# Hash attention, then a gated feed-forward: the first head prepared in two parts, and a new order for batch 0

## The chip, the cores and the metric

One core of a Trainium2 chip runs the whole program. The core has five engines with queues of their own: PE (TensorE: matrix products into PSUM), DVE (VectorE), ACT (ScalarE: exponential, Gelu, Tanh), POOL (GpSimd) and SP (SyncE, which here only issues DMA). Each engine runs its instructions in the order in which the program wrote them; between engines there are semaphores. The metric is the device time of one execution in microseconds, lower is better.

## The reference

There are four batches of eight heads, 768 tokens and 64 numbers a token. Every query and key gets six hash bits, the signs of its products with `proj`; a query attends only to the keys that have the same six bits.

```python
q_bits = (np.einsum('bhsd,dk->bhsk', q, proj) > 0).astype(np.int64)
k_bits = (np.einsum('bhsd,dk->bhsk', k, proj) > 0).astype(np.int64)
q_bucket = np.sum(q_bits * powers, axis=-1)
k_bucket = np.sum(k_bits * powers, axis=-1)
mask = q_bucket[:, :, :, None] == k_bucket[:, :, None, :]
scores = np.where(mask, scale * np.matmul(q, k.transpose(0, 1, 3, 2)), -1000000000.0)
attn = np.exp(scores - np.max(scores, axis=-1, keepdims=True))
attn = attn / (np.sum(attn, axis=-1, keepdims=True) + 1e-09)
attn_out = np.matmul(attn, v).astype(np.float32)
# x: the heads of a token side by side, 3072 x 512
ffn_out = gelu(x @ w_gate) * (x @ w_val) @ w_out
out = x + ffn_out / (1.0 + np.exp(-(x @ w_res)))
```

## The kernel before

Heads go in pairs: sixteen pairs, four to a batch. A head is 128 partitions by six stripes of 64 numbers (token = partition times six plus stripe). For a pair and a side (q or k) the steps are these. `load` brings the fp32 numbers into a tile `ld`. `tr` turns each 32 x 32 square on DVE (line 240) into a tile `t32`. The hash is a product with `proj` on PE in fp32, of which the trace shows two instructions for each product: `hash_one` does one head alone with a block-diagonal `projs` (line 298), `hash_mm` several pairs jointly (line 251). `bits_one` (lines 304 and 306), or `hash_tok` and `bits` (lines 271 and 287), turn the result back and write plus or minus a half per bit into columns 64 to 69 of a bf16 tile `nat`, beside the 64 numbers that `cast` (lines 206 to 210) put there and a constant column. PE then transposes `nat` stripe by stripe into PSUM (`turn_pe`, line 351), and `turned` copies that into `aug` (lines 358 and 360), where tokens lie along the free dimension. So a score of equal bits comes out higher than any other by a large margin, and the exponential needs no mask.

`scores(p, c)` makes one score tile of 128 x 1024 for pair p, chunk c (line 479), and ACT takes its exponential (line 490). A pair has nine chunks. Two score tiles fit in PSUM (`sc_ps`), so a score waits until the exponential two before it is done. `values` multiplies a chunk by v (line 452), and `finish` divides by the sums on DVE (lines 403 and 404) and writes `x_tok`, which is turned into `x_sb` by DMA or, for the last two pairs of batch 0, by PE (`x_turn`, line 436). Two accumulators `av_ps` exist for `hash_one`, `values` and some turns.

The feed-forward part of a batch is `gate_val` (twelve steps m of 2.6 us; two products on PE at line 503, Gelu at line 520, their product `hh` on DVE at line 523) and `project` (lines 535 and 551), which is spread over the next batch's scores.

Batch 0's attention has no earlier work to lie beside. Its order is written out by hand in the string `ORDER`: every word is a job, issued in that order on whichever engines it uses. `s7` is the score of chunk 7 counted over the batch (nine to a pair), `v7` its values, `tr31` the DVE transpose of pair 3's k, `h12` the third piece of the joint hash 1 (pairs 2 and 3), `tk1` its tokens, `bt`, `tp`, `td`, `cs` the bits, PE turn, copy and cast of a pair and side, `ld` and `lv` loads, `va` and `vs` the preparation of v on POOL, `fin31` a `finish`, `w0` to `w11` the slices of the four weight matrices (issued on POOL), `xt` an `x_turn`, `g0` and `g1` the first part of `gate_val`'s first step. `BESIDE` lists what follows each of the twelve steps m of batch 0's `gate_val`; `tu` there is a turn by DMA. Batches 1 to 3 are placed by a loop with fixed slots; with `FROM = 1` it makes the hash of half the pairs of the following batch on POOL and DVE, for b of 1 and more.

Ahead of `ORDER`, the program loads head 0 of q and k (lines 128 and 131; `projn` goes on ACT's queue between them), head 1, and then `FIRST_LOADS`, all on SP. It sets constants, runs filler products on PE (`fill`, line 174), transposes and hashes head 0 of q, then of k, and turns each (lines 564 to 586). The first score needs stripes 0 to 3 of q and stripes 0 and 1 of k; the second needs the rest of q and stripes 0 to 2 of k.

Of the kernel before, what the change touches and what calls it, by code (L numbers as in the profile page):

```python
# [9 lines left out]
FP32 = mybir.dt.float32  # L10
# [14 lines left out]
td200 v13 fin10 bt31 s17 ld51 va4 v14 s18 tr50 tp201 w0 w1 w2 bt30 td201 s19 v15 vs2 s20 tp211 cs41  # L25
td211 s21 v16 v17 cs40 s22 tr61 v18 v19 tr40 w3 s23 va3 tp310 td310 tr60 s24 v20 tp300 td300 ld70
s25 vs3 v21 tp301 td301 s26 vs4 fin11 s27 v22 v23 fin20 tr41 s28 v24 v25 s29 tp311 td311 s30 v26
# [3 lines left out]
BESIDE = [  # L31
    "h23 tk2 bt41",
    "tu41 cs61 bt40",
    "bt50",
    "tu40 cs60 ld71 tr71",
    "tr70",
    "tu50 bt51 w8 w9",
    "",
    "w10",
    "h30 h31 h32 h33 tu51 cs71 tk3 bt60 bt61 tu60 tu61",  # L40
    "pr40 rp40 bt71 tu71",
    "bt70",
    "w11 cs70 tu70",
]

@with_exitstack
def kernel(
# [44 lines left out]
    va_pool = ctx.enter_context(tc.tile_pool(name="va", bufs=4))  # L92
    e_pool = ctx.enter_context(tc.tile_pool(name="e", bufs=4))
    sm_pool = ctx.enter_context(tc.tile_pool(name="sm", bufs=2))
    sc_ps = ctx.enter_context(tc.tile_pool(name="sc_ps", bufs=2, space=PSUM))
    av_ps = ctx.enter_context(tc.tile_pool(name="av_ps", bufs=2, space=PSUM))
    mm_ps = ctx.enter_context(tc.tile_pool(name="mm_ps", bufs=1, space=PSUM))
# [27 lines left out]
        eng.dma_start(raw[p, side][:, hi * T:(hi + 1) * T].rearrange("p t d -> p (t d)"),  # L125
                      (q, k)[side][b, 2 * hp + hi].rearrange("(p t) d -> p (t d)", t=T))
# [4 lines left out]
    load_head(0, 1, 0, nc.sync)  # L131
    load_head(0, 0, 1, nc.sync)
    load_head(0, 1, 1, nc.sync)
    for what in FIRST_LOADS:
# [20 lines left out]
    def blank(i, eng):  # L155
        nat.append(const.tile([P, HT, P], BF16, name=f"nat{i}"))
        eng.memset(nat[i][:, :, D:P], 0.0)
        eng.memset(nat[i][:, :, D + NBITS:KA], 1.0 if i % 2 == 0 else -NBITS / 4.0)

    for i in range(NN):  # L160
        blank(i, nc.vector)

    def spread(dst, engs):
        for a, eng in enumerate(engs):
# [32 lines left out]
    def nat_of(x):  # L197
        return nat[(2 * x[0] + x[1]) % NN]

    def cast(p, side, eng, h0=0, h1=2):  # L200
# [8 lines left out]
        else:  # L209
            eng.tensor_copy(dst, raw[x][:, sl])  # L210

    t32, hsum, htok = {}, {}, {}
    free_banks, held_banks = ["r", "f"], {}

# [21 lines left out]
    def tr(p, side, h0=0, h1=2):  # L236
        if (p, side) not in t32:
# [2 lines left out]
        nc.vector.transpose(t32[p, side][:, sl].rearrange("p c h n -> p (c h n)"),  # L240
                            raw[p, side][:, sl].rearrange("p c d -> p (c d)"))

    def hash_mm(jobs, dhs=(0, 1), hs_=(0, 1)):
        if jobs[0] not in hsum:
            hsum[jobs[0]] = mm_ps.tile([P, HT, 32], FP32, tag=take(jobs[0]), name="hs")
        hs = hsum[jobs[0]]
        for hh in hs_:
            sl = slice(hh * T, hh * T + T)
            for dh in dhs:
                for j, x in enumerate(jobs):  # L250
                    nc.tensor.matmul(hs[32 * j:32 * j + 32, sl], projw[:, dh, :],  # L251
                                     t32[x][:, sl, dh, :], start=(dh == 0), stop=(dh == 1),
                                     tile_position=(0, 32 * j))
# [11 lines left out]
    def hash_tok(jobs, psum=False):  # L265
        n = 32 * len(jobs)
        if psum:
            ht = mm_ps.tile([P, HT, 32], FP32, tag=take(("ht", ht_of(jobs))), name="htp")
        else:
            ht = sm_pool.tile([P, HT + 3, 32], FP32, tag="ht", name="ht")  # L270
# [31 lines left out]
    def bits_one(p, side, hi):  # L302
        hs = hsum.pop((p, side, hi))
        nc.vector.transpose(hs[:, 1].rearrange("p c n -> p (c n)"),
                            hs[:, 0].rearrange("p c n -> p (c n)"))
        nc.vector.tensor_scalar(nat_of((p, side))[:, hi * T:hi * T + T, D:D + NBITS],
                                hs[:, 1, :, 0:NBITS], 0.0, 0.5, op0=ALU.is_gt, op1=ALU.subtract)
        acc_done(("hs", p, side, hi))

# [44 lines left out]
    def turned(p, side, hi, eng, t0=0, t1=T):  # L354
        dst = aug[p, side][0:KA, hi * T + t0:hi * T + t1, :]
        pt = pts[p, side, hi][0:KA, t0:t1]
        if eng is nc.scalar:
            nc.scalar.activation(dst, pt, AF.Copy)
        else:
            eng.tensor_copy(dst, pt)  # L360
        if t1 == T:
            give((p, side, hi))
            if ("pt", p, side, hi) in accs:
                acc_done(("pt", p, side, hi))

    def vals_a(p):
        vs = rawv[p]
# [161 lines left out]
    def project(b):  # L529
        hh = hidden[b]  # L530
        for t in range(T):
# [30 lines left out]


    fill(7)
    fill(1, 256)
    spread(lambda a: projs[32 * a:32 * a + 32, :, 32 * a:32 * a + NBITS],
           (nc.gpsimd, nc.scalar, nc.scalar, nc.gpsimd))
    for side in range(2):
        tr(0, side, 0, 1)
        hash_one(0, side, 0, av_ps, "av")  # L570
    cast(0, 0, nc.scalar, 0, 1)
    cast(0, 1, nc.gpsimd, 0, 1)
    bits_one(0, 0, 0)
    turn_pe(0, 0, 0)
    fill(2, 256)
    bits_one(0, 1, 0)
    turned(0, 0, 0, nc.scalar, 0, 4)
    turn_pe(0, 1, 0)
    turned(0, 1, 0, nc.vector, 0, 2)
    for side in range(2):  # L580
        cast(0, side, nc.gpsimd, 1, 2)
    cast(1, 0, nc.gpsimd)
# [61 lines left out]
    def job(name, fn):  # L644
        first[name] = fn
# [13 lines left out]
    job("tdk", lambda: turned(0, 1, 0, nc.vector, 2, T))  # L659
    job("tdq", lambda: turned(0, 0, 0, nc.vector, 4, T))  # L660
# [39 lines left out]
    FROM = 1  # L700
    PROD = (0, 0, 0, 0, 0, 1, 2, 2, 6, 7, 8, 8, 10, 10, 10, 12, 13, 13, 13, 19, 19, 20, 22, 27)
    SUMS = (1, 2, 2, 4, 5, 6, 7, 8, 9, 10, 10, 11, 12, 12, 13, 17, 19, 21, 21, 23, 23, 29, 30, 31)
    CASTS = (2, 5, 10, 11)
    VALS = (9, 6)
    LAYS = (0, 0, 3, 5)
# [4 lines left out]
    for b in range(B - 1):  # L710
        s0, p0 = b * NSLOT, (b + 1) * HP
        xs = [(p0 + i, side) for i in range(2) for side in range(2)]
        ys = [(p0 + 2 + i, side) for i in range(2) for side in range(2)]
        if b > 0:
            for j, (x, y) in enumerate(zip(xs, ys)):
                at(s0 + 24 + 2 * j, lambda x=x: tr(*x))
                at(s0 + 25 + 2 * j, lambda x=x: cast(*x, nc.gpsimd))
                loads(s0 + 2 + 4 * j, (x[0], "qk"[x[1]]))
                loads(s0 + 18 + 3 * j, (y[0], "qk"[y[1]]))
            gv(b, 0, lambda p0=p0: tokens((p0, p0 + 1), True))  # L720
            for m, x in zip(LAYS, xs):
                lay(b, m, x)
            for m, y in zip(CASTS, ys):
                gv(b, m, lambda y=y: cast(*y, nc.gpsimd))
        else:
            for m, names in enumerate(BESIDE):
                for name in names.split():
                    gv(b, m, first.pop(name))
        if b >= FROM:
            s1 = s0 + NSLOT  # L730

            def put(n, piece):
                if n < KF:
                    gv(b, n, piece)
                else:
                    at(s1 + n - KF, piece)

            plan = []
            for i, (y, j) in enumerate((y, j) for y in ys for j in range(NBITS)):
                plan.append((PROD[i] + .3, lambda y=y, j=j: part(y, j)))  # L740
                plan.append((SUMS[i] + .2, lambda y=y, j=j: part_sum(y, j)))
                if j == NBITS - 1:
                    plan.append((SUMS[i] + .2, lambda y=y: (bits_sum(y), turn(*y))))
            for n, piece in sorted(plan, key=lambda e: e[0]):
                put(int(n), piece)
    for p in range(HP, NPAIR):
        if p >= HP + 1:
            at(9 * p - VALS[0], lambda p=p: vals_s(p))
# [82 lines left out]
```

## Time and profile before

| | before |
|---|---|
| median of 3 runs | 342.24 us (340.98 to 342.32) |
| profiled execution | 342.38 us, span 340.7 us |
| PE busy | 331.5 us, 97% of the span |
| DVE, ACT, POOL busy | 217.6, 206.3, 170.1 us |
| first score on PE, first exponential on ACT | 8.77 us, 9.41 us |
| DMA, mean of the span | 126 GB/s |

Times in the views are microseconds from the start of the span. In rows of the view in order of time the columns are: start, duration, engine, line, operation, output and inputs with their shapes, number of instructions, and in brackets the idle time before them and what ended it. SPq and POOLq are queues that issue DMA. In rows of groups: busy time, mean ns of one, idle time before. In rows of waits: total, times, longest.

### The profile page before, as it was taken

The numbers are of one execution on the slowest core, as the hardware profiler recorded it, in microseconds if no ns is written. First come the engines' busy times: TensorE is split into PE (matmuls) and PEld (weight loads), VectorE is DVE, ScalarE is ACT, GpSimd is POOL, SyncE is SP. The second block draws the span as 40 slices with busy tenths as digits, with TensorE's granted clock in tenths as the row PEclk, the third lists the DMA queues.
The fourth block names the chain that finished last, engine by engine and source line by source line (L and its number), as shares of the span: only waits on it lengthen the run. The fifth ranks groups of instructions, "written<-read, shape, count | busy, mean of one in ns | idle before, by whom it ended". The sixth has DMA issues, their size and how long they took to land.

```text
span 340.7 us, 7546 instructions
## 1 busy us (share of the span) xinstructions
PE 331.5 (97%) x3012; PEld 204.2 (60%) x3060; DVE 217.6 (64%) x420; ACT 206.3 (61%) x232; POOL 170.1 (50%) x211
## 2 busy tenths in 40 slices
PE   8999999999999999999999999999999999999995
PEld 5677765555666665555666665556566665665444
DVE  5988737656343847788897675887897444333343
ACT  3689972225999972324999982223999994322220
POOL 4687940320566205998999803998998000000000
PEclk9999999999999999999999999999999999999999
DMA  7949999989786743550487932552251430000012
GB/s 239 378 104 262 171 229 163 179 137 189 178 189 186 228 102 76 101 95 2 94 204 235 258 104 85 94 93 45 48 134 48 100 56 33 31 0 2 31 63 93
DMA packets 71459, 43.09 MB, mean 126 GB/s; under 512 B 49536, under 2 KB 68480, under 8 KB 71424
## 3 DMA queue, kind: packets, MB, share of 16 engines
q1 hardware_dynamic: 65008, 37.37, 43.4%
q0 software_dynamic: 6336, 5.24, 10.5%
q8 instruction: 24, 0.39, 0.5%
q14 instruction: 11, 0.09, 0.1%
q10 hardware_dynamic: 80, 0.00, 0.0%
HBM read 29.56 MB, written 6.29 MB: 105 GB/s over the span
## 4 chain that ended last, share of the span: by engine, by line
PE 87%; ACT 4%; DVE 3%; DMA 2%; issue 2%; SPq 1%; POOL 0%; DVEq 0%
PE sp L503 32%; PE fps L551 17%; PE sp L479 17%; PE av L452 9%; PE rps L535 6%; ACT hh L490 3%; PE hs L251 2%; DVE hh L523 1%; DMA ld<-in_q_dram 1%; DMA ld<-in_k_dram 1%; PE pt L351 1%; DVE nat L287 1%; SPq L125 0%; ACT gt L520 0%; PE hs L298 0%
## 5 line engine op out<-in xcount | busy, mean ns | idle before, releaser
L490 ACT ACTIVATE e<-sp 128x1024 bf16<-128x1024 f32 x108 | 109.1, 1028 | 8.0 <-PE sp L479 2.8
L324 POOL TENSOR_TENSOR pd<-ld,prow 128x768 f32<-128x768 f32 x48 | 86.2, 1815 | 38.5 <-PE hs L251 34.4
L520 ACT ACTIVATE gt<-sp 128x768 bf16<-128x768 f32 x48 | 38.9, 811 | 90.4 <-PE sp L503 90.4
L479 PE MATMUL sp<-aug,aug 71*128 71x256 bf16 (+1 forms) x384 | 85.6, 325 | 0.8 <-DVE aug L360 0.4
L551 PE MATMUL fps<-wo,hh 128*128 128x512 bf16 (+2 forms) x288 | 74.5, 361 | 1.2
L503 PE MATMUL sp<-x_sb,wv 128*128 128x256 bf16 (+1 forms) x375 | 70.4, 324 | 1.3 <-DVE hh L523 0.8
L503 PE MATMUL sp<-x_sb,wg 128*128 128x512 bf16 (+1 forms) x375 | 70.5, 325 | 0.6
L523 DVE TENSOR_TENSOR hh<-gt,sp 128x768 bf16<-128x768 bf16 x48 | 45.8, 953 | 38.6 <-PE sp L503 34.3
L452 PEld LDWEIGHTS <-e 128*128 128x128 bf16 x864 | 40.2, 97 | 25.1
L503 PEld LDWEIGHTS <-wv 128*128 128x128 bf16 x384 | 37.5, 98 | 26.1 <-issue 1.4
L503 PEld LDWEIGHTS <-wg 128*128 128x128 bf16 x384 | 36.9, 98 | 25.7 <-issue 1.7
L328 DVE TENSOR_REDUCE hsum<-pd 128x12 f32<-128x768 f32 x48 | 44.4, 943 | 0.5
L452 PE MATMUL av<-va,e 128*128 128x65 bf16 x864 | 43.4, 193 | 0.1
L551 PEld LDWEIGHTS <-hh 128*128 128x128 bf16 x312 | 28.1, 97 | 21.8
L490 ACT ACTIVATE hh<-sp 128x1024 bf16<-128x1024 f32 x36 | 34.4, 1025 | 4.1 <-PE sp L479 3.9
L479 PEld LDWEIGHTS <-aug 71*128 71x128 bf16 x384 | 29.2, 97 | 11.6 <-issue 2.0
L554 DVE SCALAR_TENSOR_TENSOR fps<-th,fps 128x512 f32<-128x512 f32 (+2 forms) x26 | 16.9, 650 | 28.1 <-PE fps L551 26.7
L431 DVE COPY av<-av 128x390 f32<-128x390 f32 x24 | 13.7, 571 | 20.4 <-PE av L427 20.4
L535 PE MATMUL rps<-wr,x_sb 128*128 128x512 bf16 x90 | 25.9, 378 | 0.3
L210 POOL CAST nat<-ld 128x768 bf16<-128x768 f32 (+1 forms) x17 | 13.4, 788 | 24.2 <-DMA aug<-nat 23.8
L539 ACT ACTIVATE th<-rps 128x512 f32<-128x512 f32 x24 | 14.3, 594 | 18.5 <-PE rps L535 18.5
L240 DVE STREAM_TRANSPOSE t<-ld 128x768 f32<-128x768 f32 (+1 forms) x26 | 22.8, 895 | 1.6 <-DMA ld<-in_k_dram 1.4
(68 smaller groups left out, 260.1 us busy)
## 6 DMA issues: line engine op xcount, KB each, us to landing
ldv<-in_v_dram SPq DMA_DIRECT2D x16, 384.0 KB, 5.1
out_dram<-o SPq DMA_DIRECT2D x23, 256.0 KB, 2.1
ld<-in_q_dram SPq DMA_DIRECT2D x15, 384.0 KB, 4.9
ld<-in_k_dram SPq DMA_DIRECT2D x15, 384.0 KB, 5.3
wg<-in_moe_w_gate_dram POOLq DMA_DIRECT2D x4, 384.0 KB, 7.8
wv<-in_moe_w_val_dram POOLq DMA_DIRECT2D x4, 384.0 KB, 7.8
wo<-in_moe_w_out_dram POOLq DMA_DIRECT2D x3, 512.0 KB, 9.2
wr<-in_moe_w_res_dram POOLq DMA_DIRECT2D x1, 512.0 KB, 7.5
```

The source lines that it names most:

```text
L240: nc.vector.transpose(t32[p, side][:, sl].rearrange("p c h n -> p (c h n)"), raw[p, side][:, sl].rearrange("p c d -> p (c d)"))
L324: nc.gpsimd.tensor_mul(pd, raw[x], prow[:, j].unsqueeze(1).to_broadcast([P, HT, D]))
L328: nc.vector.tensor_reduce(stripes(hsum6)[:, :, :, j], hparts.pop((x, j)).rearrange("p (a c) d -> p a c d", a=3), axis=mybir.AxisListType.X ...
L452: nc.tensor.matmul(av[p, hi][:, qt, :], e[:, off:off + P], va[:, hi, jt, 0:D + 1], start=first, stop=(p >= HP and jt == T - 1), skip_group ...
L479: nc.tensor.matmul(sp[:, off:off + nq * P], ks[0:KA, hi * T + jt, :], qs[0:KA, hi * T + qt0:hi * T + qt0 + nq, :], start=True, stop=True)
L490: nc.scalar.activation(e, sp, AF.Exp, scale=float(ALPHA))
L503: nc.tensor.matmul(sp[:, c0:c1], w[:, kk, bass.ts(m, P)], xs[:, kk, c0:c1], start=(kk == 0), stop=(kk == KM - 1))
L520: nc.scalar.activation(gt, sp[:, 0:S], AF.Gelu)
L523: nc.vector.tensor_mul(hidden[b][:, m, :], gt, ps[1][:, 0:S])
L535: nc.tensor.matmul(rps, x_sb[b][:, kk, t, :], wr[:, kk, :], start=(kk == 0), stop=(kk == KM - 1))
L551: nc.tensor.matmul(fps[:, cs], hh[:, m, bass.ts(t, P)], wo[:, m, cs], start=(m == 0), stop=(m == KF - 1))
L554: nc.vector.scalar_tensor_tensor(fps[:, cs], th[:, cs], 1.0, fps[:, cs], op0=ALU.add, op1=ALU.mult)
```

## The change

- Head 0's loads are four instead of two: part A is stripes 0 to 3 of q and 0 to 1 of k, part B stripes 4 to 5 of q and 2 to 5 of k. Both parts are six stripes, so each fills one `t32` and one `hash_one`. Part A's loads go out first, then `projn`, then part B's.
- Parts are cast into a new tile `lead` instead of `nat`; both are transposed and hashed back to back, then A's bits, A's turn (in two banks), B's casts, A's copy of q on ACT, B's bits, A's copy of k on DVE. Part B's turn is the new job `tpB` in `ORDER`, its copies are `tdk` and `tdq`.
- Of the fillers, the eighth (half length) and the two between the turns go.
- Two of the four `nat` tiles are set on POOL instead of DVE, and `lead` is set on POOL.
- The hash token tile `ht` has one buffer instead of two.
- `FIRST_LOADS` puts v of pair 1 last; `ORDER` and `BESIDE` are new lists of the same jobs (with `tpB` added).
- New tables `PROD0`, `SUMS0` and `CASTS0` for b = 0 in the placing loop.

```diff
-FIRST_LOADS = [(1, "q"), (0, "v"), (1, "k"), (2, "q"), (2, "k"), (1, "v"), (2, "v"), (3, "k"), (3, "q")]
+FIRST_LOADS = [(1, "q"), (0, "v"), (1, "k"), (2, "q"), (2, "k"), (2, "v"), (3, "k"), (3, "q"), (1, "v")]
...
-trq trk s0 tdq tdk hoq bo0 ho bo1 s1 tr10 s2 tr11 tp011 td011a td011b tp001 v0 td001 v1 s3 h00 h01
-s4 cs21 h02 h03 s5 tr20 ld41 ld40 s6 v2 v3 v4 tr21 s7 tk0 bt10 bt11 tp100 tp110 td100 td110 cs20 s8
-ld50 tp111 s9 tr30 tr31 tp101 td101 fin00 s10 lv3 v5 v6 v7 v8 fin01 s11 va1 vs1 lv4 va2 s12 ld60 h10
-h11 h12 h13 ld61 td111 s13 cs31 v9 s14 v10 v11 v12 s15 cs30 tk1 bt20 bt21 tp210 s16 td210 tp200
...
-fin21 lv6 s31 lv5 cs50 v27 s32 cs51 v28 v29 s33 xt2 v30 tr51 s34 w4 w5 w6 v31 fin30 s35 gelu v32 v33
-v34 g0 v35 fin31 g1 xt3 h20 h21 h22 w7 op40
+trq tpB trk tdq s0 tdk hoq bo0 s1 tr10 ld50 ho bo1 tp001 td001 s2 tp011 td011a tr11 s3 td011b v0 v1
+cs21 tr20 s4 h00 h01 h02 h03 w0 s5 v2 v3 s6 v4 s7 tk0 bt10 bt11 tp100 tp110 td100 td110 ld40 tr31 s8
+tp111 td111 cs31 tr30 tr21 ld61 s9 tp101 td101 s10 cs20 v5 v6 v7 v8 ld41 s11 s12 h10 h11 w1 s13
+fin00 h12 h13 va2 lv3 s14 fin01 ld51 s15 va1 v9 v10 v11 tk1 bt20 bt21 bt31 s16 tp200 td200 cs30 vs1
...
+s32 v28 v29 v30 s33 xt2 s34 v31 fin30 op40 tr41 s35 gelu v32 v33 v34 g0 cs40 tr51 v35 fin31 g1 xt3
+h20 h21 cs50 w4 w5 w6 h22 tr60
...
-    "h23 tk2 bt41",
-    "tu41 cs61 bt40",
-    "bt50",
-    "tu40 cs60 ld71 tr71",
-    "tr70",
...
+    "vs4 h23 tk2 bt41 cs51",
+    "ld71 bt50",
+    "w7 tu41 cs61",
+    "tu50 bt40 tu40 cs60",
+    "w8 w9 tr71",
...
-    load_head(0, 0, 0, nc.sync)
+    PARTS = (((0, 0, 4), (1, 0, 2)), ((0, 4, T), (1, 2, T)))
...
+    def tr_part(i, side):
+        if (0, i) not in t32:
+            t32[0, i] = t32_pool.tile([P, HT, 2, 32], FP32, tag="t32", name="t32")
+        d0, d1, t0, t1 = part_of(i, side)
+        nc.vector.transpose(t32[0, i][:, d0:d1].rearrange("p c h n -> p (c h n)"),
+                            raw[0, side][:, t0:t1].rearrange("p c d -> p (c d)"))
...
+    def turn_part(i, sides, av=False):
+        what = ("part", i, sides)
+        if av:
+            acc(what)
+            pt = av_ps.tile([P, T, P], BF16, tag="av", name="pt")
+        else:
+            pt = mm_ps.tile([P, T, P], BF16, tag=take(what), name="pt")
...
     fill(7)
-    fill(1, 256)
     spread(lambda a: projs[32 * a:32 * a + 32, :, 32 * a:32 * a + NBITS],
            (nc.gpsimd, nc.scalar, nc.scalar, nc.gpsimd))
+    for i in range(2):
+        for side in range(2):
+            tr_part(i, side)
+        hash_one(0, i, 0, av_ps, "av")
+    cast_part(0, 0, nc.scalar)
+    cast_part(0, 1, nc.gpsimd)
     for side in range(2):
-        tr(0, side, 0, 1)
-        hash_one(0, side, 0, av_ps, "av")
-    cast(0, 0, nc.scalar, 0, 1)
-    cast(0, 1, nc.gpsimd, 0, 1)
+        aug[0, side] = aug_pool.tile([P, HT, P], BF16, tag=f"aug{side}", name=f"aug{side}")
     bits_one(0, 0, 0)
-    turn_pe(0, 0, 0)
-    fill(2, 256)
+    turn_part(0, (0,))
+    turn_part(0, (1,))
+    cast_part(1, 0, nc.gpsimd)
+    cast_part(1, 1, nc.gpsimd)
+    turned_part(0, 0, nc.scalar)
     bits_one(0, 1, 0)
-    turned(0, 0, 0, nc.scalar, 0, 4)
-    turn_pe(0, 1, 0)
-    turned(0, 1, 0, nc.vector, 0, 2)
+    turned_part(0, 1, nc.vector)
...
+    PROD0 = (0, 1, 2, 3, 4, 5, 6, 7, 8, 9, 10, 11, 12, 14, 16, 17, 19, 20, 22, 24, 25, 27, 28, 30)
...
-            plan = []
+            plan, prod, sums = [], PROD if b else PROD0, SUMS if b else SUMS0
```

More of the change, by code (lines that the diff above doesn't have):

```diff
@@ L126, in load_head, with load_part @@
                       (q, k)[side][b, 2 * hp + hi].rearrange("(p t) d -> p (t d)", t=T))
-    load_head(0, 0, 0, nc.sync)
+    PARTS = (((0, 0, 4), (1, 0, 2)), ((0, 4, T), (1, 2, T)))
+    def load_part(side, t0, t1):
+        if (0, side) not in raw:
+            raw[0, side] = ld_pool.tile([P, HT, D], FP32, tag=f"ld{side}", name=f"ld{side}")
+        nc.sync.dma_start(raw[0, side][:, t0:t1], (q, k)[side][0, 0].rearrange("(p t) d -> p t d", t=T)[:, t0:t1])
+    for part in PARTS[0]:
+        load_part(*part)
     projn = const.tile([32, 2, NBITS], FP32, name="projn")
     nc.scalar.dma_start(projn, proj.rearrange("(h r) n -> r h n", r=32))
-    load_head(0, 1, 0, nc.sync)
+    for part in PARTS[1]:
+        load_part(*part)
     load_head(0, 0, 1, nc.sync)
@@ L364, in turned, with turned_part @@
                 acc_done(("pt", p, side, hi))
+    part_left, part_pt = {}, {}
+    def turn_part(i, sides, av=False):
[3 more added lines that the diff above has]
+            pt = av_ps.tile([P, T, P], BF16, tag="av", name="pt")
+        else:
+            pt = mm_ps.tile([P, T, P], BF16, tag=take(what), name="pt")
+        part_left[what] = len(sides)
+        for side in sides:
+            d0, d1, _, _ = part_of(i, side)
+            for t in range(d0, d1):
+                nc.tensor.transpose(pt[0:KA, t, :], lead[:, i, t, 0:KA], ident)
+            part_pt[i, side] = (pt, what)
+    def turned_part(i, side, eng):
+        d0, d1, t0, t1 = part_of(i, side)
+        pt, what = part_pt[i, side]
+        dst, src = aug[0, side][0:KA, t0:t1, :], pt[0:KA, d0:d1]
+        if eng is nc.scalar:
+            nc.scalar.activation(dst, src, AF.Copy)
+        else:
+            eng.tensor_copy(dst, src)
+        part_left[what] -= 1
+        if part_left[what] == 0:
+            give(what)
+            if what in accs:
+                acc_done(what)
     def vals_a(p):
@@ L702 @@
     SUMS = (1, 2, 2, 4, 5, 6, 7, 8, 9, 10, 10, 11, 12, 12, 13, 17, 19, 21, 21, 23, 23, 29, 30, 31)
+    PROD0 = (0, 1, 2, 3, 4, 5, 6, 7, 8, 9, 10, 11, 12, 14, 16, 17, 19, 20, 22, 24, 25, 27, 28, 30)
+    SUMS0 = (1, 2, 3, 4, 5, 6, 7, 8, 9, 10, 11, 12, 14, 16, 18, 19, 21, 22, 24, 26, 27, 29, 30, 32)
+    CASTS0 = (3, 5, 8, 10)
     CASTS = (2, 5, 10, 11)
```

59 lines of the change are left out of this document (40 added, 19 removed).

## The prediction

> **What bounds the kernel now.** I read the page first (busy shares, the 40 slices), then the waits of PE, then the start in order of time, then the groups of the first batch, and last the stage between 56 and 66 us.
>
> ```profile
> PE 331.5 (97%) x3012; PEld 204.2 (60%) x3060; DVE 217.6 (64%) x420; ACT 206.3 (61%) x232; POOL 170.1 (50%) x211
> ...
> PE   8999999999999999999999999999999999999995
> ```
> ```profile
> PE sp L503 <- DVE hh L523: 0.8, 3, 0.4
> PE sp L479 <- DVE aug L360: 0.4, 1, 0.4
> PE sp L479 <- ACT hh L490: 0.3, 2, 0.2
> ```
>
> TensorE (PE) is full in every slice but the first and the last, and in the whole span it waits for others for under 2 us (us in total, times, longest; the fill's wait for its zeros is left out). So the time is: when dense PE work begins, plus the PE work, plus its few waits. The change leaves the PE work alone but for three fillers, and it touches only what lies before 82 us. It can win by an earlier start and by fewer waits, and lose by new waits. Here is the start:
>
> ```profile
> 0.81 0.39 SPq L125 DMA_DIRECT2D ld<-in_q_dram  x1
> ...
> 1.06 3.38 PE L174 MATMUL wps<-warm 128*128 128x512 bf16 x8 [1.06 <-POOL warm L138]
> 1.10 0.38 DVE L157 MEMSET nat<- 128x384 uint32 x1
> ...
> 1.26 0.41 SPq L125 DMA_DIRECT2D ld<-in_k_dram  x1
> ...
> 1.72 0.42 SPq L125 DMA_DIRECT2D ld<-in_q_dram  x1
> ...
> 2.19 0.43 SPq L125 DMA_DIRECT2D ld<-in_k_dram  x1
> ...
> 3.31 0.44 POOL L168 COPY projs<-projn 32x12 f32<-32x12 f32 x2 [1.45 <-DMA projn<-in_proj_dram]
> ...
> 3.46 1.04 DVE L240 STREAM_TRANSPOSE t<-ld 128x384 f32<-128x384 f32 x2
> ...
> 4.24 2.84 PE L298 MATMUL hs<-t,projs 128*128 128x192 f32 x8
> ...
> 5.84 0.40 DVE L304 STREAM_TRANSPOSE hs<-hs 128x192 f32<-128x192 f32 x1 [1.34 <-PE hs L298]
> ...
> 6.27 0.20 DVE L306 TENSOR_SCALAR nat<-hs 128x36 bf16<-128x36 f32 x1
> ...
> 6.87 0.55 PE L351 MATMUL pt<-ident,nat 128*71 128x128 bf16 x6
> ...
> 7.46 0.59 ACT L358 ACTIVATE aug<-pt 71x512 bf16<-71x512 bf16 x1 [3.13 <-PE pt L351]
> ...
> 7.89 0.50 PE L351 MATMUL pt<-ident,nat 128*71 128x128 bf16 x6 [0.25 <-POOL nat L208]
> ...
> 8.43 0.29 DVE L360 COPY aug<-pt 71x256 bf16<-71x256 bf16 x1 [0.68 <-PE pt L351]
> 8.64 1.02 DVE L240 STREAM_TRANSPOSE t<-ld 128x384 f32<-128x384 f32 x2
> ...
> 8.77 0.60 PE L479 MATMUL sp<-aug,aug 71*128 71x512 bf16 x2 [0.38 <-DVE aug L360]
> ...
> 9.35 1.54 PE L298 MATMUL hs<-t,projs 128*128 128x192 f32 x8
> ...
> 9.59 0.57 DVE L360 COPY aug<-pt 71x256 bf16<-71x256 bf16 x2
> ...
> 10.72 1.03 PE L479 MATMUL sp<-aug,aug 71*128 71x256 bf16 x6
> ...
> 15.47 1.04 PE L479 MATMUL sp<-aug,aug 71*128 71x512 bf16 x5
> ```
> ```profile
> DMA to landing us min/median/max: 2.5/2.6/2.6
> ...
> DMA to landing us min/median/max: 3.6/3.6/3.7
> ```
>
> The two landing lines are the loads of line 125, the first two issues (head 0) and the next two (head 1). The chain to the first score is load, transpose, hash of q, hash of k, k's bits, PE transpose, copy, score at 8.77. PE runs at half rate at first: eight hash passes take 2.63 us up to 6.87 (0.33 each), and the same eight 1.37 us from 9.35 (0.17 each).
>
> **The start, part by part.** Fillers: seven and a half in 3.18 us up to 4.24 is 0.42 each; without the half filler PE is free at 4.03. Loads: part A (4 stripes of q, 2 of k) goes out first; from 0.81 and 1.26 with the first two issues' 2.5 to 2.6 it lands by 3.4 and, being a third of k, between 3.4 and 3.8; I take 3.5. Transposes: 1.04 us for 12 stripes is 0.087 a stripe; A's six take 0.55, so hash A starts at 4.15 (before: 4.24).
>
> Part B is issued at 1.72 and 2.19. With 2.5 it lands at 4.7; with the 3.7 of the third and fourth issue of now, at 5.9. I take 4.7, because A and B together are the bytes that the first two issues bring now; both ends stay in the range. Then B's transposes (0.55) end at 5.25, ahead of hash A's end at 5.47 (4 x 0.33), and hold nothing. Hash B: 5.47 to 6.79. A's bits are ready earlier: DVE reads a hash 1.60 after its start (4.24 to 5.84) and needs 0.63, so 6.38. PE turns A at 6.79; ACT's copy of q (0.59) ends near 7.9. B's bits: 5.47 + 1.60 + 0.63 = 7.70; k's copy follows on DVE (0.29): 7.99. The turn of B now stands ahead of the first score on PE, at 7.81 for 0.34: first score at 8.15. That is **0.62 earlier** (ends: 0.9 with A at 3.3 and PE warm sooner, nothing with B at 5.9, where hash B starts near 6.4).
>
> But k's second part is queued on DVE behind the two transposes of head 1 (1.02) and q's second part (0.25, then 0.40): the second score can't start before 9.8, and PE has only one hash (0.65) for the 1.2 us between: a new wait of 0.55. The turn of k's head 1 waits for its bits (DVE: 0.60 after 9.75, a 0.97 transpose, 0.60: 11.95) for another 0.3. Adding PE's pieces from 9.8 up to the sixth score (three scores 0.43, hash 0.65, two turns 0.34, two value groups 0.24, the list's first joint hash 1.5) gives 15.3 against the 15.47 above: **0.17 of the 0.62 is left**.
>
> Costed at nothing: the memsets moved to POOL (two of 0.38 and six small ones) lie in POOL's 1.45 us wait for proj; without that cover the hash would move by the rest. Two more issues on SP (0.43 each) put every later load back by at most 0.9. POOL's casts of B have from its landing until 7.7, when its bits are ready; the single buffer for hash tokens is free some 7 us before the second use; the new tables PROD0, SUMS0 and CASTS0 apply to batch 0 only, which the planning loop (FROM = 1) skips.
>
> **The rest of batch 0.** From the groups and the chain:
>
> ```profile
> L490 ACT ACTIVATE hh<-sp 128x1024 bf16<-128x1024 f32 x21 | 19.8, 1027 | 0.1
> ```
> ```profile
> 22.70 1.44 PE hs L251 x32
> ...
> 27.35 0.34 PE pt L351 x6
> ...
> 28.11 0.44 PE sp L479 x3
> 28.54 0.24 PE av L452 x8
> ```
> ```profile
> L240 DVE STREAM_TRANSPOSE t<-ld 128x768 f32<-128x768 f32 x12 | 11.2, 958 | 0.1
> L360 DVE COPY aug<-pt 71x768 bf16<-71x768 bf16 x13 | 6.9, 543 | 2.2 <-PE pt L351 2.2
> ```
>
> From 27.6 to 46.3 ScalarE's exponentials follow each other without a hole, 0.92 apart (a score needs the exponential two before it), and PE fills the gaps with turns, values and hashes. I walked both lists slot by slot with these pieces against that pace (between two scores the turns, values and hashes that the list names; a score not before the exponential two before it is done). From the tenth score on that gives 1.5 us of PE waits for the old list and 1.4 for the new one, in other slots. Two new DVE queues come in. Behind the eighth score DVE has four copies (0.54) and three transposes (0.93) before the second joint hash: ready 0.3 after PE asks, of which the next waits give back 0.1: +0.2. At the end, tr41 and tr51 (0.97 each) now stand between the last two `finish` steps: the last one would end near 47.8, and PE reaches the turn that needs it between 47.45 and 47.8: +0.2 (0 to 0.4). Sum for the rest: -0.1 + 0.2 + 0.2 = +0.3, which eats the 0.17 and 0.1 more.
>
> **The feed-forward stage of batch 0.**
>
> ```profile
> 57.46 0.90 SPq L107 DMA_DIRECT2D ld<-in_k_dram  x1
> ...
> 61.68 0.98 DVE L240 STREAM_TRANSPOSE t<-ld 128x768 f32<-128x768 f32 x1 [1.40 <-DMA ld<-in_k_dram]
> 62.58 0.92 DVE L523 TENSOR_TENSOR hh<-gt,sp 128x768 bf16<-128x768 bf16 x1
> ...
> 63.55 1.46 PE L503 MATMUL sp<-x_sb,wv 128*128 128x512 bf16 x8 [0.43 <-DVE hh L523]
> 63.55 1.07 PEld L503 LDWEIGHTS <-wv 128*128 128x128 bf16 x7 [0.60 <-issue]
> ```
>
> Now the load of pair 7's k waits on SP behind a DMA transpose, its DVE transpose waits for it, the product `hh` behind that comes late, and PE stands. The new list loads it after m = 1 and transposes after m = 4, three groups of 2.6 us apart: the wait goes. PE is idle for 0.43 by its row, and its weight loads stand for 0.60, which counts the restart too: **-0.6**. What is late next: nothing, since no m carries more DVE work beside `hh` (0.95) than 1.5 us except m = 8, whose three hash pieces of DVE (2.4) lie beside a 1.4 us hash run on PE as now. The weight slices are issued earlier or, w4 to w6, a few us later than now, some 15 us before their use.
>
> **Sum.** -0.62 + 0.45 + 0.3 - 0.6 = -0.5 us. The profiled execution took 342.38 (span 340.7 and 1.7 around it), 0.14 over the median 342.24. 342.24 - 0.5 = 341.7; I round down to **341.6**, as the end's 0.2 may be nothing. The runs shown spread over 1.34 us, and eight hash passes at half rate cost 1.26 more than at full rate (2.63 - 1.37), so the spread may be the moment at which PE speeds up.
>
> **A rule against the change.** The Trainium skill, "TensorE: Matmul & The Clock Gate", Part 1, says that the array runs at half clock until a free-running window of about 3.4 us has been busy. The rows agree: half rate through the first hash, full after it. By that rule a hole in PE's work between 4 and 7 us could put full rate off by a whole window, and the sum would be +0.4 instead of -0.5, as the first rival prices it.
>
> **Rivals.** (1) Slower: part B lands at 5.9. Hash B starts near 6.4, A's bits wait behind B's transposes on DVE, PE has a hole of 0.9 just before it speeds up. If it speeds up on time the first score comes at 8.6: 342.1. If the hole delays it to about 10.4, hash, turns, first score and next hash (0.34 + 0.34 + 0.43 + 0.65, near 1.8 us at full rate) take twice as long, less the 0.55 wait that this swallows, and part of the later waits: +0.9 on top, 342.6 to 343.3. For it: the third and fourth issues took 3.6 to 3.7. Against: their bytes came behind 384 KB, B's come behind 192. It decides from a landing after 5.0.
> (2) Faster: the two DVE queues of the early list don't bind (copies finish sooner, head 1 transposes overlap) and the start's 0.62 is kept, the waits of the list fall by 0.8, and the 0.6 falls too: -2.0, 340.2. For it: PE never lacks work, only order. Against: DVE's row at 8.64 shows the same two transposes holding the second score now.
> (3) No gain: the list is paced by ACT from slot 13 on, the start's gain is lost whole, and another late transpose takes the place of the one at 61.68: 342.2 to 342.5. For it: 19.8 us of ACT with 0.1 idle. Against: three groups' distance for the load.
> (4) Slower by the third pair's loads: w0 is issued in the fifth slot instead of the nineteenth and runs beside the first loads. k3 and q3 must be there when DVE comes to them near 19.1 and 20.6; each us later delays the second joint hash by as much. Two us late: 343.8.
>
> **Chances.** Forecast (341.1 to 342.1) 0.44, rival 1 0.19, rival 2 0.18, rival 3 0.10, rival 4 and other new waits of its kind 0.09. The range 340.4 to 343.4 leaves out half of rival 2 and the far ends of 1 and 4. About 0.5% (1.7 us) is what a measurement of this kernel tells from no change: below 340.5 most of rival 2, 0.15; above 343.9 the far ends, 0.17 with what I have overlooked in so long a list; between, 0.68.
>
> **What would show it.** In the profile after: hash A near 4.15 and eight passes without a hole; first score near 8.15, second near 9.8 with an idle PE before it; the joint hash of pairs 2 and 3 waiting for DVE's transpose; the x_tok turn near 48 waiting for `finish`; no PE wait near 63. Wrong would be: a hole between the hashes, full rate only after 10 us, PE waits of over 0.5 us in the list, or unchanged waits for `hh`.

## The result, and the profile after

The changed kernel takes 345.12 us (median, 344.71 to 347.22) against 342.07 us for the kernel before in the same job: ratio 1.0103, interval 1.0074 to 1.0131. It is 3 us slower, where 0.5 us faster was forecast, and lies above the range. The profiled execution took 344.71 us, 2.33 more than that of before, with a span of 343.0 (before 340.7). The times below are from these two profiles where nothing else is said.

| us from the start of the span | before | after | difference |
|---|---|---|---|
| first score on PE | 8.77 | 7.69 | -1.08 |
| first exponential | 9.41 | 8.32 | -1.09 |
| ninth exponential | 19.01 | 18.58 | -0.43 |
| last exponential of batch 0 | 45.46 | 44.93 | -0.53 |
| first Gelu | 50.40 | 49.88 | -0.52 |
| seventh Gelu | 66.34 | 65.24 | -1.10 |
| tenth Gelu | 75.69 | 74.62 | -1.07 |
| twelfth Gelu | 80.92 | 81.82 | +0.90 |
| first exponential of batch 1 | 83.04 | 83.95 | +0.91 |
| twelfth exponential of batch 1 | 95.39 | 97.36 | +1.97 |
| span | 340.7 | 343.0 | +2.3 |

At 75 us the changed kernel is a full microsecond ahead. Two places turn that round: 2.0 us between the tenth and the twelfth Gelu, and 1.1 us in batch 1's first scores. The last 0.3 us arise at the very end, behind the last products, and stay unexplained.

The page of after, busy times and the slices of PE:

```profile
PE 332.9 (97%) x3057; PEld 203.0 (59%) x3057; DVE 216.9 (63%) x418; ACT 206.4 (60%) x232; POOL 172.1 (50%) x221
...
PE   7999999997999999999999999999999999999995
```

The busy times are those of before within 2 us; the first slice has gone from eight to seven, and the tenth (77 to 86 us) has lost its nine. PE's waits of after (us in total, times, longest):

```profile
PE sp L572 <- DVE hh L592: 2.2, 3, 1.8
...
PE av L496 <- POOL vsum L450: 0.9, 1, 0.9
PE pt L390 <- POOL nat L325: 0.5, 1, 0.5
PE pt L418 <- DVE lead L345: 0.5, 1, 0.5
PE hs L336 <- DVE t L278: 0.4, 1, 0.4
```

The first two rows are the two places. First the start, in order of time:

```profile
1.81 0.73 POOL L167 MEMSET nat<- 128x768 bf16 x1
...
3.22 0.64 DVE L278 STREAM_TRANSPOSE t<-ld 128x256 f32<-128x256 f32 x2 [1.00 <-DMA ld<-in_q_dram]
...
3.63 0.43 POOL L189 COPY projs<-projn 32x12 f32<-32x12 f32 x2
...
4.12 0.85 PEld L336 LDWEIGHTS hs<-t,projs 128*128 128x128 f32 x4 [0.79 <-POOL projs L189]
4.12 1.14 PE L336 MATMUL hs<-t,projs 128*128 128x192 f32 x4
...
5.13 0.45 DVE L278 STREAM_TRANSPOSE t<-ld 128x256 f32<-128x256 f32 x1 [0.57 <-DMA ld<-in_k_dram]
...
5.63 0.92 PE L336 MATMUL hs<-t,projs 128*128 128x192 f32 x4 [0.36 <-DVE t L278]
...
7.36 0.50 PE L418 MATMUL pt<-ident,lead 128*71 128x128 bf16 x6 [0.48 <-DVE lead L345]
...
7.69 0.60 PE L548 MATMUL sp<-aug,aug 71*128 71x512 bf16 x2
...
8.78 0.60 PE L548 MATMUL sp<-aug,aug 71*128 71x256 bf16 x3
```

Hash A starts at 4.12 (forecast 4.15), released by POOL's copy of `projs`, which ends at 4.06; part A has been transposed since 3.86. Part B's k lands at 5.10, so hash B waits 0.36 us. The trace's record of the granted clock (the share of full speed that PE is given) begins with full rate, at 4.61; in before it begins at 6.97. The products agree: the four passes of hash A take 1.14 us, those of hash B 0.92. So the first score comes 0.46 us before the forecast. Of this start's 1.09 us, 0.66 is given back by the ninth exponential, in a place that the prediction didn't name:

```profile
15.50 0.96 POOL L214 DMA_DIRECT2D wg<-in_moe_w_gate_dram  x1
...
16.54 0.99 POOL L325 TENSOR_SCALAR nat<-ht 32x72 bf16<-32x72 f32 x2
...
17.58 0.53 PE L390 MATMUL pt<-ident,nat 128*71 128x128 bf16 x6 [0.51 <-POOL nat L325]
```

The weight load `w0`, now in the fifth slot, costs POOL 0.96 us to issue; POOL's half of the next bits stands behind it, and PE's turn behind those.

Now the place at 77 us, in order of time:

```profile
66.05 21.73 SPq L378 DMA_TRANSPOSE aug<-nat  x4
...
74.62 0.81 ACT L589 ACTIVATE gt<-sp 128x768 bf16<-128x768 f32 x1 [3.33 <-PE sp L572]
...
77.00 0.98 DVE L325 TENSOR_SCALAR nat<-htp 32x72 bf16<-32x72 f32 x4 [2.18 <-DMA aug<-nat]
77.09 0.82 POOL L231 CAST nat<-ld 128x768 bf16<-128x768 f32 x1 [10.26 <-issue]
...
77.86 1.48 POOL L214 DMA_DIRECT2D wo<-in_moe_w_out_dram  x2
78.02 0.95 DVE L592 TENSOR_TENSOR hh<-gt,sp 128x768 bf16<-128x768 bf16 x1
...
79.03 1.46 PE L572 MATMUL sp<-x_sb,wv 128*128 128x512 bf16 x8 [1.84 <-DVE hh L592]
```

DVE stands for 2.18 us at `bt71`, which writes bits into a `nat` tile. The new list has `bt71` after step 8; in the old one it stood after step 9, and DVE came to it at 78.51:

```profile
78.51 0.98 DVE L287 TENSOR_SCALAR nat<-htp 32x72 bf16<-32x72 f32 x4
```

There are four `nat` tiles, and this one is still being read by `tu51`, the DMA transpose of pair 5's k. It was issued at 66.05 and landed 10.9 us later, at 76.98. Behind `bt71` on DVE is the product `hh`, which has its Gelu since 75.43, and behind `hh` is PE. The landing of `tu51`, first in after, then in before (there it was issued at 67.1):

```profile
DMA to landing us min/median/max: 10.9/10.9/10.9
```
```profile
DMA to landing us min/median/max: 7.6/7.6/7.6
```

In before it landed at 74.7, almost four microseconds before DVE came to `bt71`. It lands later now because two weight slices go out with it, as the second experiment shows. POOL's rows of after, then of before:

```profile
64.49 0.83 POOL L229 TENSOR_SCALAR nat<-ld 128x768 bf16<-128x768 f32 x1 [5.60 <-DMA aug<-nat]
65.28 0.81 POOL L214 DMA_DIRECT2D wr<-in_moe_w_res_dram  x1
66.08 0.75 POOL L214 DMA_DIRECT2D wo<-in_moe_w_out_dram  x1
```
```profile
60.55 0.81 POOL L193 DMA_DIRECT2D wr<-in_moe_w_res_dram  x1
61.35 1.50 POOL L193 DMA_DIRECT2D wo<-in_moe_w_out_dram  x2
74.91 0.82 POOL L210 CAST nat<-ld 128x768 bf16<-128x768 f32 x1 [12.06 <-DMA aug<-nat]
```

`w8` and `w9` stand in the list a step earlier than before, and are issued 4.7 us later: on POOL they queue behind `cs60`, which waits until `tu40` has read its tile. `w10` (the first of the two at 77.86) comes some 16 us later than before, where it was the second of the two at 61.35: it now queues behind `cs71`, which waits for `tu51` (10.26 us idle; 12.06 in before, with only `w11` behind it).

The second place, batch 1's first scores:

```profile
87.83 0.58 SPq L355 DMA_DIRECT2D pn<-in_proj_dram  x1
...
91.85 0.87 POOL L359 COPY prow<-pn 128x384 f32<-128x384 f32 x1 [11.64 <-DMA pn<-in_proj_dram]
92.70 0.99 POOL L446 TENSOR_TENSOR v<-ldv 128x384 f32<-128x384 f32 x1
...
94.69 0.11 POOL L450 MEMSET vsum<- 128x2 bf16 x1
...
94.85 0.19 PE L496 MATMUL av<-vsum,eps_sb 128*128 128x65 bf16 x1 [0.91 <-POOL vsum L450]
```

The rows of `proj` (`pn`) go out on SP behind the turns; SP issues them at 87.83 (before: 84.0). POOL comes to their copy `prow` 11.64 us before they land, and everything behind it on POOL waits with it, among it the sums of v of pair 5, which PE needs. In before POOL stood about as long, but the copy came 3.5 us earlier, and PE had no wait for the sums:

```profile
88.35 0.87 POOL L320 COPY prow<-pn 128x384 f32<-128x384 f32 x1 [11.05 <-DMA pn<-in_proj_dram]
```

### The profile page after: what moved, and what is told of

The parts are those of the page before. It is cut to its first block, busy times and chain, and to the rows that moved or that the text cites. A ratio compares the mean times of both kernels' runs of the same rounds, so it can differ in the third digit from the quotient of the medians.

```text
span 343.0 us, 7601 instructions
## 1 busy us (share of the span) xinstructions
PE 332.9 (97%) x3057; PEld 203.0 (59%) x3057; DVE 216.9 (63%) x418; ACT 206.4 (60%) x232; POOL 172.1 (50%) x221
## 4 chain that ended last, share of the span: by engine, by line
PE 86%; DVE 3%; ACT 2%; DMA 1%; SPq 1%; POOL 1%; issue 1%; DVEq 0%
PE sp L572 34%; PE fps L620 17%; PE sp L548 16%; PE av L521 9%; PE rps L604 6%; PE hs L289 2%; DVE hh L592 2%; DMA pn<-in_proj_dram 1%; ACT hh L559 1%; PE pt L390 1%; SPq L378 1%; DVE nat L325 1%; ACT gt L589 0%; DVE hsum L367 0%; PE pt L505 0%
## 5 line engine op out<-in xcount | busy, mean ns | idle before, releaser
L620 PE MATMUL fps<-wo,hh 128*128 128x512 bf16 (+2 forms) x312 | 79.5, 362 | 0.0
L572 PE MATMUL sp<-x_sb,wv 128*128 128x512 bf16 (+1 forms) x384 | 70.9, 326 | 2.2 <-DVE hh L592 2.2
L620 PEld LDWEIGHTS <-hh 128*128 128x128 bf16 x312 | 28.1, 97 | 22.9 <-issue 1.2
L604 PE MATMUL rps<-wr,x_sb 128*128 128x512 bf16 x96 | 27.1, 379 | 0.0
L271 DVE STREAM_TRANSPOSE t<-ld 128x768 f32<-128x768 f32 (+1 forms) x24 | 22.0, 925 | 0.1
```

The source lines that it names most:

```text
L572: nc.tensor.matmul(sp[:, c0:c1], w[:, kk, bass.ts(m, P)], xs[:, kk, c0:c1], start=(kk == 0), stop=(kk == KM - 1))
L604: nc.tensor.matmul(rps, x_sb[b][:, kk, t, :], wr[:, kk, :], start=(kk == 0), stop=(kk == KM - 1))
L620: nc.tensor.matmul(fps[:, cs], hh[:, m, bass.ts(t, P)], wo[:, m, cs], start=(m == 0), stop=(m == KF - 1))
```

## The experiments

The theories that the quoted expectations letter are about three questions. What makes the wait at 77 us: the order (A: `bt71` ahead of the moment at which its tile is free), the traffic (B: `w8` and `w9` beside the turn), or both together. What makes the wait at 94 us: a follow-up of the first, or the rows of `proj` on SP alone (C). And which part of the change holds the loss: the lists (D), or, as the rival, the new start (E). The kernel before has a median of 341.09 us beside the first four, 341.63 beside the next four (25 runs, 340.80 to 342.77) and 341.36 beside the last.

**The swap undone.** `bt71` goes back behind step 9, `bt60` before step 9.

```diff
-    "h30 h31 h32 h33 tk3 bt61 bt71 tu61 tu71",
-    "bt60 tu60",
+    "h30 h31 h32 h33 tk3 bt61 bt60 tu61 tu60",
+    "bt71 tu71",
```

> One swap in the changed kernel's list beside the feed-forward steps: after step 8 the bits of pair 6 (both sides), after step 9 those of pair 7's k (the changed kernel has pair 7's k after step 8). Theory A, DVE stands at pair 7's k bits because the tile that they overwrite is still read by the DMA transpose of pair 5's k (tu51, landed at 76.98), and the product hh behind them on DVE holds PE: the wait of 1.84 us at 79.0 goes, 2.0 us less than the changed kernel, near 343.1; the wait at 94.85 stays or shrinks. Rival B, the late transposes hold the step wherever the bits stand: no more than 0.5 us less, with a wait after step 9 instead.

345.29 us, ratio 1.0116 (1.0091 to 1.0141). The wait at 77 us is gone, and the twelfth Gelu is at 79.92, 1.00 ahead of before. So the mechanism there is as read. The time isn't won: PE now waits 1.9 us in batch 1 for a slice of `wo` (the row is `PE fps L620 <- DMA wo`), and runs 3.41 us at half rate afterwards. The wait at 94 us doesn't come up: `pn` goes out at 82.62 here.

**The weights `w8` and `w9` three steps later**, after step 7 instead of 4.

```diff
-    "w8 w9 tr71",
+    "tr71",
...
-    "w10 w11 pr40 rp40",
+    "w8 w9 w10 w11 pr40 rp40",
```

> The changed kernel with the weight loads w8 and w9 issued after step 7 instead of step 4. Rival B, the transpose tu51 lands late (10.9 us after its issue, others 3.7 to 4.6) because wr and the first slice of wo were issued on POOL in the 0.8 us around it and share its DMA engines: tu51 lands by 71, the wait at 79.0 goes though the bits stay where they are, 2.0 us less, near 343.1. If the weights have nothing to do with it: tu51 lands near 77 as now and the time stays near 345.

348.36 us, ratio 1.0213 (1.0181 to 1.0245). The same `tu51`, with `bt71` left early, now lands

```profile
DMA to landing us min/median/max: 4.1/4.1/4.1
```

after its issue at 65.9, and there is no wait at 77 us (twelfth Gelu 79.64). That shows that the two weight loads make the 10.9. With the first run it also shows that the wait at 77 us needs both, the order and the traffic: either change alone takes it away. But the four slices now go out together, at 70.8 to 73.9; the next two transposes, issued at 74.8 and 79.8, take 12.8 and 10.4 us to land. `pn` goes out on SP behind them, at 89.63, and PE's longest wait is

```profile
PE av L496 <- POOL vsum L450: 3.4, 1, 3.4
```

It ends at 96.11, and from 94.44 on PE runs for two windows of 3.41 us at half rate. The traffic has to go somewhere.

**The rows of `proj` after step 3 instead of 9.**

```diff
-    gv(0, 9, lambda: pn.append(rows()))
+    gv(0, 3, lambda: pn.append(rows()))
```

> The changed kernel with the load of the proj rows (pn) issued after step 3 instead of step 9. Theory C, PE's wait of 1.1 us at 94.85 is for pair 5's sums of v on POOL, which stand behind the copy of the proj rows, which waits for pn, which waits on SP behind three DMA transposes: the wait at 94.85 goes, the wait at 79.0 stays: 1.1 us less than the changed kernel, near 344.0. Rival: pair 5's sums are late for POOL's own backlog (casts and weight issues): wait stays, near 345.

345.31 us, ratio 1.0119 (1.0097 to 1.0141). No wait for `vsum` is left, so theory C holds for the place at 94 us: the rows' place behind the turns makes that wait. Whether it needs the late turns of the first place too isn't told apart: with the swap undone the rows kept their place and no wait arose, but PE was held for `wo` shortly before. The wait at 77 us stays (2.41 us), and a half-rate window follows it.

**Both, the swap undone and the rows early.**

> Both moves, of the bits and of the proj rows. If A and C hold: the two waits go, 3.1 us less than the changed kernel, 342.0, and, as the start and the wait at 63 of the kernel before are won, about 1 us below the kernel before, 341.0 to 341.3. If one wait only moves: 343 to 344.

344.57 us, ratio 1.0103 (1.0087 to 1.0119). Both waits are gone, and batch 1 begins at 81.80, 1.24 ahead of before. Then PE waits for `wo`. POOL's rows, and PE's in order of time:

```profile
77.39 0.82 POOL L231 CAST nat<-ld 128x768 bf16<-128x768 f32 x1 [10.70 <-issue]
78.16 1.48 POOL L214 DMA_DIRECT2D wo<-in_moe_w_out_dram  x2
```
```profile
85.91 0.38 PE L620 MATMUL fps<-wo,hh 128*128 128x512 bf16 x1 [1.93 <-DMA wo<-in_moe_w_out_dram]
```

The slices `w10` and `w11` were held on POOL behind `cs71`, which stood 10.70 us until `tu51` landed. In after the same slices landed at 84.3 and 87.8; the wait for them lay hidden under the one at 77 us. What follows on PE, by windows (us, busy time of PE, PEld, DVE, ACT and POOL, granted clock, DMA share, GB/s):

```profile
83.26:86.67 3.41, 1.48 (x16) 0.81 (x15) 0.00 (x0) 1.89 (x3) 3.25 (x9) 1.00 1.17 170
86.67:90.08 3.41, 3.41 (x20) 1.68 (x19) 0.00 (x0) 1.73 (x2) 0.42 (x2) 0.50 1.70 230
90.08:93.49 3.41, 3.36 (x40) 2.13 (x39) 1.72 (x3) 2.65 (x4) 0.00 (x0) 1.00 0.48 141
```

The hole of 1.93 us is followed by one window at half the clock: 20 products where the next window has 40. Half of 3.41 us is some 1.7 us more. So -1.24 + 1.93 + 1.7 gives +2.4 of the +2.8 in span; 0.3 of the rest is the unexplained end.

**The lists alone**, in the kernel before (old start; `ORDER`, `BESIDE` and `FIRST_LOADS` of the changed kernel).

> The new lists (FIRST_LOADS, ORDER, BESIDE) with the old start: head 0 in two loads, one hash after the other, the fillers of the kernel before. Theory D, all the loss sits in the list beside the feed-forward steps, and the two-part start is a gain of its own that reaches only about 0.5 us behind the first batch: DVE's stand at pair 7's k bits as in the changed kernel, 345 to 346, no better than the changed kernel. Rival E, the two-part start is what upsets the later order (its earlier first score moves everything against the loads): near 342.

345.49 us, ratio 1.0118 (1.0097 to 1.0138). The loss is all there, with the same first wait:

```profile
PE sp L503 <- DVE hh L523: 2.7, 3, 2.3
```

**The start alone**, in the changed kernel (the old lists, with `tpB` put first).

> The two-part start with the old lists (the turn of part B put in front of them). Theory D: 0.3 to 1 us below the kernel before, no wait near 77 or 93. Rival E: slower than before. It also shows whether PE comes to full rate near 4.6 to 5.7 us, as in the five profiles with the two-part start so far, or as late as 7.0, as in the profile of the kernel before.

341.49 us, ratio 0.9997 (0.9985 to 1.0009). Rival E falls: the new start costs nothing. It also wins nothing that can be told. Its first score is at 7.03, and the first Gelu at 49.89, as in after; the old wait for `hh` is there (0.49 us up to 63.10, with weight loads standing for 0.67).

**The changed kernel with the old order beside steps 1 to 11**, `ld71` early:

```diff
-    "ld71 bt50",
-    "w7 tu41 cs61",
-    "tu50 bt40 tu40 cs60",
-    "w8 w9 tr71",
-    "bt51",
-    "tr70 lv6 tu51 cs71",
-    "w10 w11 pr40 rp40",
-    "h30 h31 h32 h33 tk3 bt61 bt71 tu61 tu71",
-    "bt60 tu60",
+    "ld71 w7 tu41 cs61 bt40",
+    "bt50",
+    "tu40 cs60 tr71",
+    "tr70",
+    "tu50 bt51 w8 w9",
+    "lv6",
+    "w10",
+    "h30 h31 h32 h33 tu51 cs71 tk3 bt60 bt61 tu60 tu61",
+    "pr40 rp40 bt71 tu71",
...
-    "cs70 tu70",
+    "w11 cs70 tu70",
```

> The changed kernel with the jobs beside the feed-forward steps put back to the old steps (turn and cast of pair 5's k after step 8, the third slice of wo issued before them; the k load of pair 7 stays early, after step 1). Theory D, refined: the loss needs the cast of pair 5's k (it waits for a DMA transpose) to stand ahead of the wo slices on POOL, or its nat tile to be wanted after step 8. With both undone no PE wait of over 0.6 us between 60 and 100, and the gains of the start and of the early k load stay: 1 to 1.3 us below the kernel before.

341.54 us, ratio 1.0006 (0.9995 to 1.0017). The whole loss is in these strings. None of the late waits is left; `hh` costs PE what it cost before, less the wait at 63 us:

```profile
PE sp L572 <- DVE hh L592: 0.4, 2, 0.2
```

The gain expected here did show in the profile (span 339.7, batch 1 at 81.75), but not in the medians.

**All weights early in the new list** (`w8` and `w9` after step 1, `w10` after 4, `w11` after 7, swap undone, rows early).

```diff
-    "ld71 bt50",
-    "w7 tu41 cs61",
+    "ld71 w7 w8 w9 bt50",
+    "tu41 cs61",
...
-    "w8 w9 tr71",
+    "w10 tr71",
...
-    "w10 w11 pr40 rp40",
+    "w11 pr40 rp40",
```

> The new list kept, with one idea: wr and two slices of wo are issued on POOL after step 1 and 4, ahead of the casts that wait for DMA transposes, the last slice after step 7; pair 7's k bits after step 9, the proj rows loaded after step 3. If the weights' place behind those casts is the cause of the wait near 84 in the run with both moves: no wait there, no half-rate window after it, 1 to 1.5 us below the kernel before. If the DMA engines are simply too full there: a wait for a weight slice or for a turn remains, 342 to 344.

342.86 us, ratio 1.0044 (1.0013 to 1.0075). Its profile has none of the holes (span 339.9, time 341.56), but the runs go from 341.38 to 345.83. The two longest, 345.46 and 345.83, have a mean granted clock of 0.995 and 0.993, the profiled one 1.000. One window of 3.41 us at half rate in 340 us takes 0.005 off the mean, so in those two a hole seems to have opened and half-rate windows to have followed; 343.79 came with 1.000, longer without such a window. This order is near an edge; what tips it wasn't seen.

**The start alone, with the load of pair 7's k after step 1.**

```diff
-    "tu41 cs61 bt40",
+    "ld71 tu41 cs61 bt40",
...
-    "tu40 cs60 ld71 tr71",
+    "tu40 cs60 tr71",
```

> The two-part start with the old lists, and one job moved: pair 7's k is loaded after step 1 of batch 0's feed-forward stage instead of step 3. If PE's wait near 62.3 (0.66 us in the run with the start alone) is for that load, it goes: 0.6 us below that run, 340.9, 0.2% below the kernel before.

340.92 us, ratio 0.9986 (0.9977 to 0.9994), the best of all and below both kernels, if by only 0.4 us. Its waits for `hh` are 0.4 in all.

**That load moved in the kernel before, nothing else.**

> The kernel before with that one job moved. The wait of 0.43 us at 63.55 goes: 0.6 us below the kernel before. If the two-part start is worth nothing, this run and the one with both tie; if it is worth the 0.5 us that its first feed-forward step shows (49.89 against 50.40), this run is that much slower.

341.27 us, ratio 0.9992 (0.9980 to 1.0004). The wait at 63 us is gone and batch 1 begins at 82.16, 0.9 ahead of before in the profile; in the medians it is 0.1, which can't be told from none. The run with both moves is 0.35 us shorter in the median (340.92); its runs reach from 340.44 to 341.43, those of this run from 340.44 to 342.24. So it stays open whether the new start is worth something beside the moved load.

**The kernel before, profiled twice more.**

> The kernel before, a second profile. Its runs fall into two clusters, near 341.0 and near 342.2. If the clusters are the moment at which PE comes to full rate, a profile near 341.0 shows full rate well before 7.0 us and the later stages shifted by about 1.2 us as one; if not, the shift arises at some wait later on.

> The kernel before, a third profile, for the same question: what separates the two clusters of its runs.

342.23 and 342.31 us, full rate at 6.92 and 7.01 us, and the wait near 63 us is 0.34 and 0.33. All three profiles of before lie in the upper part of its runs (340.83 to 342.38 in this job, median 341.36). So a gain of 1 us read against these profiles is partly their own place in the spread, and what the shorter runs of before do otherwise stays open.

## Why the prediction was wrong, point by point

**The failed step** stands in the feed-forward part: "What is late next: nothing, since no m carries more DVE work beside `hh` (0.95) than 1.5 us except m = 8". That adds up DVE's work in each step; what it left out is what a moved piece waits for. `bt71` needs a `nat` tile back from a DMA transpose, `cs60` and `cs71` likewise, and the row that told it was in the trace of before: POOL stood 12.06 us for `DMA aug<-nat` at `cs71`. In its place the runs showed 2.0 us at 77 us (one swap undone takes it away), 1.1 us at 94 us (the rows of `proj` earlier take that away), and behind both a third wait for `wo` that appears when they are gone. With this fell the premise that the change "touches only what lies before 82 us": the second place lies at 94 us, and the wait for `wo` near 84.

**The weights.** "The weight slices are issued earlier or, w4 to w6, a few us later than now, some 15 us before their use" was read from the lists. By the rows `w8` and `w9` are issued 4.7 us later and `w10` 16 us later, because POOL's queue stands at the casts ahead of them. The place in a list gives the order on a queue, not the time.

**The start.** Hash A at 4.12 met the forecast of 4.15, but not by the step that was to set it: part A was transposed at 3.86, not 4.05, and by the trace the hash waited for POOL's copy of `projs`. The memsets were costed at nothing because they "lie in POOL's 1.45 us wait for proj". On POOL each of the two takes over 0.7 us and not 0.38; they outlast that wait, and the copy begins at 3.63 instead of 3.31. That this cost nothing is luck: it ends at 4.06, about when the fillers leave PE free (4.03 in the forecast). The first score was right in mechanism and came 0.46 early: the term for half-rate products was too large, as full rate came at 4.61 and not after 6.8. In two runs with the new start where it came at 6.81 (the early load) and 6.96 (the old order beside the steps), the first score is at 8.14 and 8.19, as forecast. Part B landed at 5.10 at the latest (taken: 4.7; ends 4.7 and 5.9), with a wait of 0.36 before hash B. The second score came at 8.78, not 9.8: DVE came to head 1's transposes at 7.33 and to the two copies behind them at 8.28, some 0.7 us earlier than in the forecast's walk, so the 0.55 us wait did not arise.

"0.17 of the 0.62 is left" at the sixth score was mis-sized. The pieces listed for it add up to 14.4 (14.7 with the wait of 0.3), not to 15.3, so by its own terms nothing was lost there. By the rows nothing was: the sixth exponential starts at 15.00, against 16.12 before. The loss came behind it, at the turn at 17.58 behind `w0`, which costs 0.67 from start to start. How early the first score comes hardly reaches the first Gelu: the start alone, after, the early load and the old order beside the steps have their first scores at 7.03, 7.69, 8.14 and 8.19, and their first Gelu at 49.89, 49.88, 49.92 and 49.70.

**The wait at 63 us** goes, as predicted: -0.6 was forecast, -0.58 more lies between the first and the seventh Gelu. The two runs that move the load of pair 7's k alone show that this one word does it.

**The turn of `x_tok` near 48** had no wait of note, and neither had the joint hash of pairs 2 and 3, so the +0.2 forecast for each was nothing.

**The rivals.** (1) did not occur: there was no delay of full rate, and the start alone is level with before. The Trainium skill's rule that was weighed there ("TensorE: Matmul & The Clock Gate", Part 1) bears on this case all the same, at 80 to 100 us instead of at the start: the half-rate stretches are 3.41 us long, as that section gives the window. What sends PE back to half rate is read from the runs' own windows, in the last section. (2) was right that the early DVE queues don't bind, and right on the 63 us wait; it left the late waits out. (3) "another late transpose takes the place of the one at 61.68" came nearest, something late on DVE ahead of `hh`; but the late one was a DMA transpose, and it cost 2 us where the rival priced only the gain not won. (4) named late loads, but of pair 3's q and k, for which PE never waited; `w0` did cost, through POOL's time to issue it.

**The chances** did not fit each other. Of the rivals only (4), with 0.09 for it and its kind, came near 343.8, yet 0.17 was put above 343.9 for what the list might hide; the measured time lies there.

**The size.** By the profiles: -1.07 up to the tenth Gelu, +2.0, +1.1 and +0.3 make +2.3. The medians differ by 3.05. The runs of after spread from 344.71 (mean clock 0.999) to 347.22 (0.993); 0.006 of 343 us is 2 us of clock, a little over one half-rate window's worth, which the profiled run of after was spared. That isn't all that parts the runs: in the lists alone, two runs with a mean clock of 1.000 took 345.50 and 345.62, no less than the two with 0.995 (345.20 and 345.48).

## What to carry to other kernels

Before a piece of work is moved ahead in a hand-made order, look up what gives its tile back: if a DMA transpose reads that tile, its landing time under the traffic of that stage decides, not the piece's own duration. A load issued on an engine that also waits for tiles leaves when that engine's oldest wait ends, so give weight loads a place ahead of such waits, or read their issue times from the trace. And take one wait away at a time while reading what stands behind it: here three lay under each other, and the waits of 1.88 us and more each brought a half-rate window on top of their own length.

## What the runs showed of the hardware

- Holes of 1.88 to 2.41 us in PE's work were followed by one window of 3.41 us at half the clock (the swap undone, both, the lists alone, the rows alone), the hole of 3.44 us by two windows (the weights later); the hole of 1.84 us in after by none. In windows of 3.41 us, PE was busy for 1.01 (the rows alone), 1.18 (the lists alone), 1.48 (both), 1.53 (the swap undone) and 1.65 us (the weights later) in those ahead of half rate, and for 1.57 us in the one of after that was not; none of them was idle throughout. So in these runs the edge lies near half busy, and is not sharp. One such window costs some 1.7 us, an estimate: half of 3.41 us in which PE is busy throughout.
- The same DMA transpose `tu51` took 4.1, 7.6, 8.8 and 10.9 us to land, in the kernel with the weights later, before, the old order beside the steps, and after. With the weights later, the two behind it took 12.8 and 10.4 us.
- Full rate came between 4.19 and 7.01 us over the profiles, by the start of the clock record: 4.19 to 6.96 with the new start, 5.32 to 7.01 with the old one. The rows agree: the same eight hash passes took 1.70 us in the start alone (4.19) and 2.88 with the early load (6.81). As the fillers were the same within each kind, they do not set the moment alone.
